# Ninety-six scatters that wait for TensorE, and centroid products and gate logits in column groups

## The chip, the cores and the metric

The kernel runs on one core of one Trainium2 chip. A core has TensorE (PE; its weight loads are listed apart as PEld), VectorE (DVE), ScalarE (ACT), GpSimd (POOL) and SyncE (SP), each with its own queue of instructions, and 16 DMA engines. The metric is the time of one execution on the device in microseconds, lower being better. All inputs and the output are float32.

## The reference

The reference is a chain of three parts. The third takes its gate and its skip score from the second's output.

```
q_assign = argmax(q_n @ c_n, -1)                 # q_n, k_n, c_n: rows of length 1; 16 centroids per head
k_assign = argmax(k_n @ c_n, -1)
mask = q_assign[:, :, :, None] == k_assign[:, :, None, :]
scores = where(mask, q @ k.T / sqrt(64), -1e9)   # 2 batches, 8 heads, 768 tokens, head size 64
attn = softmax(scores) @ v
x = attn, heads side by side                     # 1536 tokens of 512
h = x @ w_in                                     # 512 -> 2048
x = where(h > 0, h, exp(h) - 1) @ w_out          # 2048 -> 512
skip_score = x @ w_skip                          # only tokens with a score above 0 go on, the others are copied
logits = x @ w_gate                              # 8 experts
e = argmax(logits); gate_w = softmax(logits)[e]
out = x + gate_w * (relu(x @ w1[e]) @ w2[e])     # 512 -> 1024 -> 512
```

## The kernel before

**Heads go in pairs**, two heads of 64 on 128 partitions, four pairs for each batch. The two batches are worked in different ways.

Batch 0 is *dense*: its four pairs (n = 0 to 3) compute all 768 x 768 scores, and the mask is added by rows of one-hot clusters under the head's 64 rows. Its steps in the order table are `scores`, `peak`, `exp`, `flip` (three transposes of the exponentials by PE into one bank, L519), `head` (ACT rounds them to fp32r, `ptH`, L531), `rest` (DVE subtracts that from them, `ptL`, L537), `pv` (the products with V). ACT's `head` needs PE's `flip`, DVE's `rest` needs `head`, and the next `flip` into the same bank needs `rest`.

Batch 1 is *sorted*: for each of its four pairs (j = 0 to 3) the rows of q, k and v are put in the order of their clusters, so that later only blocks near the diagonal are computed. The clusters come from centroid products (`sort_similar`, L712 to 718), the largest of 16 (`sort_max`), running sums (`scum`, `srank`) and an index for each token (`sidx`). Then 24 indirect DMAs per pair, issued by POOL, write each token's row to its place in DRAM: `sort_scatter`, L767 to 776, steps `sc0a` to `sc5d`, for chunks of 128 tokens (0 to 5), q or k with v, head 0 or 1, into the tensors `qs` and `kvs`. That makes 96 scatters. Before them SP fills `kvs` with zeros (`zero`), and SP loads the rows (`sload`); behind the last ones the sorted rows are read back (`bload0` to `bload7`) and the block attention runs (`tq` to `nm`), whose results 48 gathers on POOL bring back to token order (`og`, L868).

**The order is written out by hand.** `attention()` (L1131) goes through a table ORDER of 1902 step names ("sc3a:0" is a scatter of pair 0, "head2b:1" a `head` of dense pair 1) and calls each step's function; each engine gets its instructions in the order in which the steps stand. The table holds everything up to the second half of the FFN (`cv`, `h`, `e`, `y`, `z` steps: weights split into two parts, products, ELU). A scatter stands 1 to 47 steps behind the one before. Between engines only data dependencies make anyone wait; a scatter waits for its index, its row load, the zero fill and the scatter eight ahead of it on its DMA semaphore.

**Centroid products of the dense pairs.** `similar` (L393 to 401) multiplies q and k by the centroids in three fp32r passes (`cwH` times the head `T[nm, "H"]` and the rest `T[nm, "L"]`, `cwL` times the head), for each half of the tokens: 12 matmuls of 64 columns of weights and 384 moving columns, L399. `similar_out` copies each half to `rows`, and `turn_back` (L405) transposes six pieces of 64 rows. A bank then holds, for each chunk of 128 tokens, four groups of 16 similarities (L408).

**Centroid products of the sorted pairs.** `sort_similar` takes the turned tokens as weights (128 columns) and the 32 centroid columns `cwF` as what moves: 12 float32 matmuls, L716, straight into the layout that `sort_max` reads.

**The gate.** `route` takes each tile of 128 FFN output tokens, turns it (`turn`, L1445) and multiplies it by `wgs` (gate and skip weights, 16 columns): `logits`, L1449 to 1454, four float32 matmuls into one 128 x 16 accumulator and a copy by DVE. For batch 1's last tiles the steps stand in a second table, TAIL: T turns, L makes logits, C chooses the expert, R ranks, h is held back work of TensorE (the last FFN products), x fetches tokens, F fills slots. The routed experts follow (L1683 to 1768).

Of the kernel before, what the change touches and what calls it, by code (L numbers as in the profile page):

```python
# [10 lines left out]
F32 = mybir.dt.float32  # L11
# [23 lines left out]
TAIL = ("h3 h3 h3 T0 T2 h3 L0 T1 h5 L2 L1 T3 h5 C0 h4 h4 R0 h4 h4 x- T4 h5 L3 L4 C3 h5 x0 T5 R3 x2 L5 x4 F0 C5 R5 N5 x3 x1 x5 F5 F3").split()  # L35
# [8 lines left out]
NEAR = 4  # L44
BY_DVE = 16, 16
# [4 lines left out]
    turnq0:0 THq0:0 turnq1:0 TLq0:0 THq1:0 turnk0:0 TLq1:0 THk0:0 turnk1:0 TLk0:0 THk1:0 TLk1:0 simq0:0 simk0:0 loadqk:0 sT0:0  # L50
    simq1:0 simk1:0 sT1:0 back:0 sv:0 mx:0 eqsub:0 turnq0:1 rawq0:1 first:0 THq0:1 turnq1:1 TLq0:1 least:0 rawq1:1 THq1:1
    equal:0 TLq1:1 rows:0 moveT0:0 moveO0:0 oT:0 turnk0:1 rawk0:1 THk0:1 moveT1:0 turnk1:1 TLk0:1 rawk1:1 THk1:1 TLk1:1 vtH:0
    vtL:0 sload0:0 sload1:0 bank scores0a:0 scores0b:0 scores1b:0 peak0:0 exp0:0 scores1a:0 scores2a:0 peak1:0 scores2b:0
    flip0a:0 exp1:0 flip0b:0 head0a:0 scores3a:0 head0b:0 peak2:0 rest0a:0 scores3b:0 rest0b:0 flip1a:0 moveO1:0 flip1b:0 exp2:0
    head1a:0 scores4a:0 peak3:0 scores4b:0 head1b:0 rest1a:0 exp3:0 suq0:0 pv0a:0 flip2a:0 rest1b:0 pv0b:0 head2a:0 flip2b:0
    pv0c:0 rest2a:0 scores5a:0 seq0:0 suq1:0 head2b:0 peak4:0 scores5b:0 seq1:0 peak5:0 flip3a:0 simq0:1 exp4:0 simk0:1 pv0d:0
    zero:0 scores6b:0 sT0:1 suk0:0 rest2b:0 head3a:0 flip3b:0 pvlow0:0 rest3a:0 pvsum0:0 scores6a:0 sek0:0 flip4a:0 head3b:0
    simq1:1 exp5:0 rest3b:0 simk1:1 peak6:0 head4a:0 sT1:1 flip4b:0 rest4a:0 scores7a:0 suk1:0 loadv:0 head4b:0 flip5a:0
    scores7b:0 sek1:0 back:1 exp6:0 rest4b:0 sv:1 flip5b:0 peak7:0 sload0:1 scores8a:0 mx:1 scores8b:0 head5a:0 ssim0:0 eqsub:1
    ssim1:0 pv1a:0 rest5a:0 pv1c:0 peak8:0 pv1b:0 flip6a:0 pv1d:0 head5b:0 exp7:0 scores9b:0 first:1 exp8:0 rest5b:0 scores10a:0  # L60
    least:1 smx:0 vtH:1 flip6b:0 sone:0 head6a:0 pvlow1:0 scum:0 srank:0 pvsum1:0 pv2a:0 rest6a:0 flip7a:0 pv2c:0 equal:1 pv2b:0
    head7a:0 vtL:1 pv2d:0 moveT0:1 scores9a:0 sidx:0 rows:1 head6b:0 rest6b:0 flip7b:0 sc2c:0 rest7a:0 pvlow2:0 peak9:0 oT:1
    flip8a:0 loadqk:1 head7b:0 pvsum2:0 rest7b:0 exp9:0 scores10b:0 turnq0:2 peak10:0 pv3a:0 pv3b:0 pv3c:0 scores11b:0 sc3b:0
    scores11a:0 sc4b:0 THq0:2 TLq0:2 flip8b:0 turnq1:2 sc0d:0 head8a:0 sc5a:0 rest8a:0 exp10:0 moveO0:1 flip9a:0 head8b:0
    scores0a:1 peak11:0 THq1:2 head9a:0 scores0b:1 rest8b:0 pv3d:0 TLq1:2 flip9b:0 rest9a:0 exp11:0 turnk0:2 flip10a:0 head9b:0
    rest9b:0 pvlow3:0 pvsum3:0 scores1b:1 scores1a:1 head10a:0 flip10b:0 sc0a:0 pv4a:0 rest10a:0 flip11a:0 THk0:2 peak0:1
    sload1:1 sc3a:0 TLk0:2 pv4b:0 pv4c:0 head10b:0 rest10b:0 head11a:0 exp0:1 pv4d:0 suq0:1 seq0:1 flip11b:0 scores2a:1 sc2d:0
    sc1b:0 pvlow4:0 rest11a:0 flip0a:1 turnk1:2 peak1:1 pvsum4:0 head11b:0 THk1:2 exp1:1 rest11b:0 TLk1:2 scores2b:1 pv5a:0
    peak2:1 invert:0 head0a:1 pv5b:0 flip0b:1 suq1:1 zero:1 pv5c:0 scores3a:1 seq1:1 sc4d:0 scores3b:1 simq0:2 head0b:1 rest0a:1
    exp2:1 sc2a:0 simk0:2 sc1a:0 flip1a:1 rest0b:1 peak3:1 flip1b:1 scores4a:1 sT0:2 head1a:1 scores4b:1 rest1a:1 moveT1:1  # L70
    suk0:1 exp3:1 sc5b:0 pv5d:0 flip2a:1 sc1c:0 peak4:1 moveO1:1 sek0:1 loadv:3 head1b:1 scores5a:1 sc5c:0 simq1:2 sc0b:0 smem:0
    simk1:2 head2a:1 exp4:1 rest1b:1 scores5b:1 flip2b:1 scores6b:1 sT1:2 head2b:1 rest2a:1 loadv:1 pvlow5:0 suk1:1 flip3a:1
    peak5:1 scores6a:1 rest2b:1 sc1d:0 sek1:1 flip3b:1 back:2 sumT:0 exp5:1 scores7a:1 pvsum5:0 sc2b:0 head3a:1 peak6:1 rest3a:1
# [91 lines left out]
class _Core:  # L165
# [26 lines left out]
    def first_loads(self):  # L192
# [1778 lines left out]
```

## Time and profile before

| | |
|---|---|
| time, median of 3 runs | 749.87 us (747.6 to 751.81) |
| the profiled execution | 748.56 us |
| its span on the core | 746.8 us |
| PE busy | 635.4 us, 85% |
| PEld busy | 576.0 us, 77% |
| DVE busy | 431.6 us, 58% |
| ACT busy | 392.9 us, 53% |
| POOL busy | 271.7 us, 36% |
| mean granted clock of TensorE | 0.921 |

The profile is one execution. Its span runs from the first to the last instruction; the execution's own time is 1.8 us more. Busy shares are means over stages that differ: attention, FFN and experts. The granted clock is the share of TensorE's full clock that the chip allowed.

### The profile page before, as it was taken

How to read it: one execution, taken by the hardware profiler on the slowest of the kernel's cores; microseconds unless marked ns; L12 is line 12 of the kernel's file. 1: busy time of each engine (PE TensorE's matmuls, PEld its weight loads, DVE VectorE, ACT ScalarE, POOL GpSimd, SP SyncE). 2: the span in 40 equal slices, each digit the busy share in tenths (PEclk: the TensorE clock that was granted, in tenths of full speed). 3: DMA queues.
4: the chain of work that ended last, by engine and by line, in shares of the span. 5: the costliest groups of instructions: out<-in, count | busy, mean ns of one | idle time of the engine just before them, and what ended most of it. 6: DMA issues, size and time to landing. Idle time of an engine off the chain costs nothing.

```text
span 746.8 us, 11604 instructions
## 1 busy us (share of the span) xinstructions
PE 635.4 (85%) x3988; PEld 576.0 (77%) x3988; DVE 431.6 (58%) x982; ACT 392.9 (53%) x850; POOL 271.7 (36%) x289
## 2 busy tenths in 40 slices
PE   5991892874772399999999999999999999999996
PEld 3881882773662399888989889999998988999995
DVE  6680790872660398999698775333245545135663
ACT  4761770852641398776776765544544622124552
POOL 3247067047057302865664352323223203121101
PEclk9795896897695599999999999999999999999999
DMA  7877064576331039666654553642421027989960
GB/s 174 208 172 195 14 156 112 129 159 165 91 90 37 22 101 251 183 178 199 204 180 154 165 161 101 254 169 61 165 57 57 14 110 266 384 291 319 335 231 18
DMA packets 99957, 118.30 MB, mean 158 GB/s; under 512 B 47553, under 2 KB 68209, under 8 KB 99888
## 3 DMA queue, kind: packets, MB, share of 16 engines
q1 hardware_dynamic: 92080, 106.70, 47.4%
q0 software_dynamic: 6096, 10.34, 4.3%
q8 instruction: 33, 0.54, 0.3%
q10 hardware_dynamic: 1712, 0.43, 0.3%
q14 instruction: 36, 0.29, 0.1%
HBM read 80.17 MB, written 27.80 MB: 145 GB/s over the span
## 4 chain that ended last, share of the span: by engine, by line
PE 65%; DVE 11%; another core or an unknown queue 11%; ACT 6%; issue 3%; DMA 1%; SPq 0%; POOL 0%; POOLq 0%; ACTq 0%; DVEq 0%
PE ps_p L1269 7%; PE ps_v L1269 6%; PE ps_t L1720 5%; PE ps_t L519 4%; PE ps_p L1735 4%; PE ps_v L1735 4%; PE ps_v L550 4%; PE ps_sB L1308 3%; PE ps_sA L1308 3%; PE ps_t L1308 3%; PE ps_sA L498 2%; PE ps_sB L498 2%; PE ps_sA L1325 2%; DVE cv_b L1217 1%
## 5 line engine op out<-in xcount | busy, mean ns | idle before, releaser
L519 PE MATMUL ps_t<-ident,pe 128*128 128x128 f32 x288 | 53.5, 307 | 59.9 <-issue 30.4
L519 PEld LDWEIGHTS ps_t<-ident,pe 128*128 128x128 f32 x288 | 38.6, 159 | 66.8 <-issue 32.8
L531 ACT ACTIVATE ptH<-ps_t 128x384 fp32r<-128x384 f32 x96 | 46.0, 491 | 82.5 <-remote 59.0
L537 DVE TENSOR_TENSOR ptL<-ps_t,ptH 128x384 fp32r<-128x384 f32 x96 | 52.1, 551 | 58.9 <-ACT ptH L531 45.7
L868 POOL DMA_INDIRECT og<-od,idx x48 | 51.2, 1066 | 55.2 <-ACT rp L830 27.8
L1223 POOL TENSOR_TENSOR r<-cv_b,cv_t 128x512 int32<-128x512 int32 x32 | 42.9, 1341 | 47.5 <-DVE cv_b L1217 19.7
L550 PE MATMUL ps_v<-ptH,vt 128*128 128x256 f32 x144 | 44.0, 328 | 14.6 <-issue 8.6
L1269 PE MATMUL ps_p<-xH,w1H 128*128 128x384 f32 x128 | 44.3, 346 | 1.9 <-DVE gL L1297 1.5
L1768 POOL DMA_INDIRECT out_dram<-o,dest x10 | 11.0, 1104 | 93.4 <-DVE o L1766 92.8
L1293 DVE SCALAR_TENSOR_TENSOR ps_p<-e,ps_p 128x384 f32<-128x384 f32 x32 | 17.9, 560 | 45.1 <-ACT e L1291 45.1
L550 PEld LDWEIGHTS ps_v<-ptH,vt 128*128 128x128 f32 x144 | 30.7, 215 | 16.6 <-issue 9.3
L1269 PE MATMUL ps_v<-xH,w1H 128*128 128x384 f32 x124 | 42.0, 339 | 1.3 <-DVE gL L1297 1.3
L1269 PE MATMUL ps_p<-xL,w1H 128*128 128x384 f32 x128 | 43.0, 336 | 0.0
L550 PE MATMUL ps_v<-ptL,vt 128*128 128x256 f32 x144 | 41.5, 312 | 0.3 <-DVE ptL L537 0.3
L1269 PE MATMUL ps_v<-xL,w1H 128*128 128x384 f32 x124 | 41.6, 335 | 0.0
L1249 POOL TENSOR_TENSOR w2L<-r,w2H 128x512 fp32r<-128x512 f32 x12 | 15.3, 1279 | 71.5 <-PE ps_t L1308 57.4
L1289 ACT ACTIVATE e<-ps_p 128x384 f32<-128x384 f32 x32 | 15.7, 490 | 40.7 <-PE ps_p L1269 40.7
L770 POOL DMA_INDIRECT kvs<-rowsH,idx x24 | 23.8, 990 | 33.8 <-DVE idx L755 23.1
L1735 PE MATMUL ps_p<-xs,ew 128*128 128x128 f32 (+2 forms) x256 | 35.4, 280 | 0.5 <-ACT xs L1683 0.5
L1735 PEld LDWEIGHTS ps_p<-xs,ew 128*128 128x128 f32 x256 | 33.7, 191 | 2.3 <-ACT xs L1683 0.6
L1735 PEld LDWEIGHTS ps_v<-xs,ew 128*128 128x128 f32 x256 | 33.7, 191 | 1.8
L1735 PE MATMUL ps_v<-xs,ew 128*128 128x128 f32 (+2 forms) x256 | 35.0, 279 | 0.0
(491 smaller groups left out, 2006.7 us busy)
## 6 DMA issues: line engine op xcount, KB each, us to landing
ew<-in_moe_w_dram SPq DMA_DIRECT2D x32, 1024.0 KB
d<-in_moe_w_in_dram SPq DMA_DIRECT2D x16, 512.0 KB
d<-in_moe_w_out_dram SPq DMA_DIRECT2D x16, 512.0 KB
wf_d<-r SPq DMA_DIRECT2D x16, 512.0 KB
r<-wf_d SPq DMA_DIRECT2D x16, 512.0 KB
zk<-kvs SPq DMA_DIRECT2D x8, 520.0 KB
KA<-kH SPq DMA_DIRECT2D x16, 192.0 KB
kvs<-zeros SPq DMA_DIRECT2D x8, 325.0 KB
```

Of the source, the lines that this page charges most:

```text
L498: self.nc.tensor.matmul(self.sc[u][:, half, 0:384], lhsT=d["Q" + a][0:rows, c * 128:c * 128 + 128], rhs=d["K" + a][0:rows, half * 384:half ...
L519: self.nc.tensor.transpose(ps[:, 0, j * 128:j * 128 + 128], self.pe[u][:, half, j * 128:j * 128 + 128], self.ident)
L531: self.nc.scalar.activation(self.split(u, half)[0], self.tp[u, half][:, 0, 0:384].rearrange("p (c q) -> p c q", c=3), AF.Copy)
L537: self.nc.vector.tensor_tensor(l, self.tp.pop((u, half))[:, 0, 0:384].rearrange("p (c q) -> p c q", c=3), h.bitcast(F32), ALU.subtract)
L550: self.nc.tensor.matmul(self.vp[n, j], lhsT=self.vt[n][:, j // NG, c, :], rhs=t, start=(part == 0 and i == 0), stop=(part == 3 and i == 2 ...
L770: store = self.nc.gpsimd.indirect_dma_start(dst[2 * j + h], bass.IndirectOffsetOnAxis(ap=self.idx[:, j, 4 * c + r:4 * c + r + 1], axis=0), ...
L868: self.nc.gpsimd.indirect_dma_start(self.og[j][:, c, h, :], None, self.o_d[i], bass.IndirectOffsetOnAxis(ap=self.idx[:, j, 4 * c + h:4 * c ...
L1223: G.tensor_tensor(r[:, j * 512:j * 512 + 512].bitcast(I32), b, self.cvt.pop((f, j)), ALU.add)
L1269: self.nc.tensor.matmul(ps, lhsT=w[:, c, :], rhs=x[:, c, :], start=(i == 0), stop=(i == 11))
L1308: self.nc.tensor.matmul(self.y[bl][part][t], lhsT=a[:, t * 128:t * 128 + 128], rhs=w, start=(f == 0 and i == 0), stop=(f == NF - 1 and i = ...
L1720: PE.matmul(y[0][0:W], lhsT=a, rhs=b, start=(f == 0 and i == 0), stop=(f == NF - 1 and i == 2))
L1735: PE.matmul(ps[:, 0:W], lhsT=w1[:, c, i * 128:i * 128 + 128], rhs=xs[:, c, 0:W], start=(c == 0), stop=(c == 3))
```

## The change

**A wait for each scatter.** `sort_scatter` calls a new function `follow`, which makes the scatter depend on the TensorE instruction that stands fourteen TensorE instructions ahead in the flat order of the program (FOLLOW = 14).

**A new table.** ORDER is written anew: 1890 steps. The scatters now stand 5 to 22 steps apart, 9 or 10 mostly. Everything around them moves a little too: zero fills, row loads, V's low part, the centroid steps.

**Centroid products in four column groups.** A dense pair's twelve matmuls become eight with the float32 centroids `cwF` (32 columns) as weights: q and k of both halves go to four different quarters of the partitions of one bank, head first, then rest on top. One copy (`similar_out`, to `simT`) and three full transposes follow, where there were two and six. A sorted pair's twelve matmuls become four of the same form with the turned tokens moving, a copy by ACT (`sTT`) and three transposes (`sback`). The groups of 16 similarities stand in another order afterwards, and `group` and `index` say where. `cwH` and `cwL` go.

**Gate logits in four column groups.** Each of the four pieces of a turned tile is multiplied into its own quarter, with the weights `wgs`, now 32 wide, loaded and 128 tokens moving. A copy, one transpose and a sum over the four quarters by DVE (`back`, steps B0 and B3 in TAIL) follow, held over to the next tile. The last tile of batch 1 keeps the old form. `second_ops` asks for the low weights of the second FFN product only where they are used.

```diff
 TAIL:
-"h3 h3 h3 T0 T2 h3 L0 T1 h5 L2 L1 T3 h5 C0 h4 h4 R0 h4 h4 x- T4 h5 L3 L4 C3 h5 x0 T5 R3 x2 L5 x4 F0 C5 R5 N5 x3 x1 x5 F5 F3"
+"h3 h3 h3 T0 T2 h3 L0 T1 h5 L2 h5 L1 T3 h4 B0 C0 h4 h4 h4 x- R0 T4 h5 L3 h5 L4 x0 B3 C3 T5 x2 L5 R3 x4 F0 C5 R5 N5 x3 x1 x5 F5 F3"
+FOLLOW = 14
 ORDER = """
...
-    sload1:1 sc3a:0 TLk0:2 pv4b:0 pv4c:0 head10b:0 rest10b:0 head11a:0 exp0:1 pv4d:0 suq0:1 seq0:1 flip11b:0 scores2a:1 sc2d:0
...
+    pvsum3:0 exp11:0 turnk0:2 rest10a:0 pv4a:0 sc4d:0 moveO1:1 peak0:1 pv4b:0 THk0:2 pv4c:0 head10b:0 flip11a:0 TLk0:2 zero:1
...
-    def similar(self, n, nm, half):
...
-        for j, (w, x) in enumerate(((self.cwH, "H"), (self.cwH, "L"), (self.cwL, "H"))):
-            self.nc.tensor.matmul(self.sim[n, half][0:64, 0:384], lhsT=w[:, p, o:o + 64], rhs=self.T[n][nm, x][:, cs],
-                                  start=(nm == "q" and j == 0), stop=(nm == "k" and j == 2))
...
+    def similar(self, n):
...
+        for x in "HL":
+            for i, (half, nm) in enumerate(itertools.product(range(2), "qk")):
+                self.nc.tensor.matmul(ps[32 * i:32 * i + 32, 0:384], lhsT=self.cwF[:, p, :],
+                                      rhs=T[nm, x][:, half * 384:half * 384 + 384].bitcast(F32), start=(x == "H"), stop=(x == "L"))
+
+    def similar_out(self, n):
+        self.simT = self.sort_tile("sT", [128, 384], F32)
+        self.nc.scalar.activation(self.simT, self.sim.pop(n)[:, 0:384], AF.Copy)
...
     def turn_back(self, n):
         ps = self.back[n] = self.bank_p()
-        for c in range(self.NC):
-            self.nc.tensor.transpose(ps[:, c * 64:c * 64 + 64], self.rows[0:64, c * 128:c * 128 + 128], self.ident[0:64, 0:64])
+        for c in range(3):
+            self.nc.tensor.transpose(ps[:, c * 128:c * 128 + 128], self.simT[:, c * 128:c * 128 + 128], self.ident)
...
-        for c in range(3 * half, 3 * half + 3):
-            for i, nm in enumerate("qk"):
-                o = c * 64 + 32 * i
-                self.nc.tensor.matmul(self.ssim[:, o:o + 32], lhsT=self.sT[j, nm][:, c * 128:c * 128 + 128],
-                                      rhs=self.cwF[:, j, :], start=True, stop=True)
+    def sort_similar(self, j):
+
+        ps = self.ssims = self.bank_p()
+        for i, (half, nm) in enumerate(itertools.product(range(2), "qk")):
+            self.nc.tensor.matmul(ps[32 * i:32 * i + 32, 0:384], lhsT=self.cwF[:, j, :],
+                                  rhs=self.sT[j, nm][:, half * 384:half * 384 + 384], start=True, stop=True)
...
+    def group(self, c):
+        return c % 3 * 8 + c // 3 * 4
+
+    def index(self, j, c, r):
+        g = self.group(c) + r
+        return self.idx[:, j, g:g + 1]
+
     def sort_scatter(self, j, c, r):
...
         store = self.nc.gpsimd.indirect_dma_start(
-            dst[2 * j + h], bass.IndirectOffsetOnAxis(ap=self.idx[:, j, 4 * c + r:4 * c + r + 1], axis=0),
+            dst[2 * j + h], bass.IndirectOffsetOnAxis(ap=self.index(j, c, r), axis=0),
             self.sort_rows(j, c // 3)[:, c % 3, lo:hi], None, bounds_check=1023, oob_is_err=False)
+        self.follow(store)
...
+    def follow(self, store):
+
+        done = [i for i in self.nc.cur_bb.bb.instructions if i.engine == mybir.EngineType.PE][-FOLLOW]
+        self.tc.add_manual_dep(store.ins, done.name, mybir.DependencyInfo(mybir.DependencyClass.Sync, mybir.DependencyReason.DATA),
+                               reason="scatters keep step with TensorE")
...
         def logits(t):
...
             for j in range(4):
-                PE.matmul(lp, lhsT=x2T[:, j * 128:j * 128 + 128], rhs=self.wgs[:, j, :],
-                          start=(j == 0), stop=(j == 3))
-            V.tensor_copy(lg[:, t, :], lp)
+                PE.matmul(lp[32 * j:32 * j + 32, 0:128], lhsT=self.wgs[:, j, :], rhs=x2T[:, j * 128:j * 128 + 128],
+                          start=True, stop=True)
+            before = back(lp)
+            lgT = fw.tile([128, 128], F32, tag="lgT", bufs=2, name="lgT")
+            (S.copy if b else V.tensor_copy)(lgT, lp[:, 0:128])
+            held["back"] = t, lgT
+            before()
```

**POOL, before, the end of the scatters of pair 0 and the start of pair 1's.** `qs` and `kvs` are the sorted tensors in DRAM, `rowsH` and `rowsL` the loaded rows, DMASW a scatter of POOL itself, DMAHW a load or fill of SP, `eq` the similarities of a dense pair and `vt` the low part of V:

```order
L770 DMA qs_191<-rowsH,idx 1024x64 [waits DMASW1_49]
L770 DMA kvs_198<-rowsH,idx 1024x130 [waits DMASW2_49]
L429 TENSOR_TENSOR eq<-eq,mx 128x384 [waits DVE_49]
L770 DMA kvs_199<-rowsL,idx 1024x130 [waits DMASW3_49]
L770 DMA qs_190<-rowsL,idx 1024x64 [waits DMASW4_49]
L490 TENSOR_TENSOR vt<-natv,vt 128x12x64 [waits DMAHW2_49,DMAHW3_49,PE_49,Activation_49]
L770 DMA kvs_198<-rowsL,idx 1024x130 [waits DMASW5_49]
L770 DMA kvs_199<-rowsL,idx 1024x130 [waits DMASW6_49]
L770 DMA kvs_198<-rowsL,idx 1024x130 [waits DMASW7_49]
L770 DMA kvs_200<-rowsL,idx 1024x130 [waits DMAHW1_49,DMAHW0_49,DMAHW7_49,DMASW0_49,DVE_49]
L770 DMA qs_193<-rowsL,idx 1024x64 [waits DMAHW0_49,DMASW1_49]
L770 DMA kvs_201<-rowsH,idx 1024x130 [waits DMAHW1_49,DMASW2_49]
```

**POOL, after, the same place:**

```order
L778 DMA kvs_195<-rowsH,idx 1024x130 [waits DMASW7_49,PE_49]
L778 DMA kvs_195<-rowsH,idx 1024x130 [waits DMASW0_49,PE_49]
L778 DMA kvs_194<-rowsL,idx 1024x130 [waits DMASW1_49,PE_49]
L425 TENSOR_TENSOR eq<-eq,mx 128x384 [waits DVE_49]
L778 DMA qs_187<-rowsL,idx 1024x64 [waits DMASW2_49,PE_49]
L778 DMA qs_187<-rowsL,idx 1024x64 [waits DMASW3_49,PE_49]
L778 DMA kvs_194<-rowsH,idx 1024x130 [waits DMASW4_49,PE_49]
L778 DMA qs_186<-rowsH,idx 1024x64 [waits DMASW5_49,PE_49]
L778 DMA qs_187<-rowsH,idx 1024x64 [waits DMASW6_49,PE_49]
L778 DMA qs_186<-rowsL,idx 1024x64 [waits DMASW7_49,PE_49]
L486 TENSOR_TENSOR vt<-natv,vt 128x12x64 [waits DMAHW3_49,DMAHW2_49,Activation_49]
L778 DMA qs_188<-rowsH,idx 1024x64 [waits DMAHW5_49,DMASW0_49,DMAHW6_49,DVE_49,PE_49]
```

Each scatter carries a wait for PE now, beside the waits that it had. The subtraction of the largest similarity (L429, now L425) and V's low part (L490, now L486) stand among the scatters as before.

**PE, before, the centroid products of the first dense pair**, behind the transposes of its q and k (`ps_p`, `ps_v`, `ps_t` are banks of PSUM):

```order
L399 MATMUL ps_p<-qH,cwH 64x384 [waits DVE_49]
L399 MATMUL ps_p<-qL,cwH 64x384
L399 MATMUL ps_p<-qH,cwL 64x384
L399 MATMUL ps_p<-kH,cwH 64x384 [waits Activation_49]
L399 MATMUL ps_p<-kL,cwH 64x384 [waits DVE_49]
L399 MATMUL ps_p<-kH,cwL 64x384
L399 MATMUL ps_v<-qH,cwH 64x384 [waits PE_49]
L399 MATMUL ps_v<-qL,cwH 64x384
L399 MATMUL ps_v<-qH,cwL 64x384
L399 MATMUL ps_v<-kH,cwH 64x384 [waits Activation_49]
L399 MATMUL ps_v<-kL,cwH 64x384 [waits DVE_49]
L399 MATMUL ps_v<-kH,cwL 64x384
```

**PE, after, the same place**, with the three transposes back:

```order
L394 MATMUL ps_p<-qH,cwF 32x384 [waits DVE_49]
L394 MATMUL ps_p<-kH,cwF 32x384 [waits Activation_49]
L394 MATMUL ps_p<-qH,cwF 32x384
L394 MATMUL ps_p<-kH,cwF 32x384 [waits Activation_49]
L394 MATMUL ps_p<-qL,cwF 32x384
L394 MATMUL ps_p<-kL,cwF 32x384 [waits DVE_49]
L394 MATMUL ps_p<-qL,cwF 32x384
L394 MATMUL ps_p<-kL,cwF 32x384 [waits DVE_49]
L404 MATMUL ps_v<-ident,ssT 128x128 [waits Activation_49]
L404 MATMUL ps_v<-ident,ssT 128x128 x2
```

Twelve matmuls of 64 columns of weights in two banks became eight of 32 columns in one bank; the six transposes of L408 that stood behind them became three.

## Rows read from the trace of the kernel before

**Rows 1.** The page's chain that ended last, shares of the span by engine.

```profile
PE 65%; DVE 11%; another core or an unknown queue 11%; ACT 6%; issue 3%; DMA 1%; SPq 0%; POOL 0%; POOLq 0%; ACTq 0%; DVEq 0%
```

**Rows 2.** The table of stretches, busy time of each engine in each stretch.

```profile
core 0: us, PE busy (x) PEld busy (x) DVE busy (x) ACT busy (x) POOL busy (x), PEclk, DMA share, GB/s
...
49.00:75.50 26.50, 9.77 (x60) 7.90 (x59) 6.87 (x12) 6.52 (x14) 18.66 (x19) 0.67 0.63 167
75.50:106.80 31.30, 29.10 (x206) 27.00 (x206) 27.25 (x56) 23.12 (x53) 7.73 (x7) 0.89 0.37 86
106.80:132.00 25.20, 10.42 (x63) 8.91 (x63) 6.78 (x13) 6.72 (x15) 17.75 (x18) 0.69 0.38 102
132.00:168.00 36.00, 30.76 (x208) 27.88 (x209) 29.33 (x59) 25.39 (x57) 8.50 (x8) 0.89 0.63 149
168.00:192.00 24.00, 9.69 (x60) 8.15 (x58) 5.66 (x11) 5.73 (x12) 15.57 (x16) 0.70 0.69 177
192.00:211.50 19.50, 18.21 (x122) 17.15 (x122) 16.55 (x35) 14.69 (x35) 0.00 (x0) 0.84 0.12 29
211.50:254.00 42.50, 12.07 (x71) 10.25 (x70) 9.57 (x20) 8.05 (x17) 30.13 (x31) 0.62 0.21 65
254.00:280.00 26.00, 25.56 (x198) 24.05 (x198) 21.25 (x56) 22.01 (x53) 1.05 (x2) 0.89 0.28 72
...
305.00:600.00 295.00, 289.69 (x1554) 260.32 (x1553) 184.49 (x360) 177.97 (x359) 126.56 (x104) 1.00 0.44 141
600.00:746.00 146.00, 138.89 (x1018) 129.28 (x1018) 68.13 (x212) 50.58 (x124) 21.32 (x20) 0.99 0.70 250
```

**Rows 3.** The timeline of 50 to 80 us: start, duration, engine, work, [idle before].

```profile
61.73 0.90 PE L519 MATMUL ps_t<-ident,pe 128*128 128x128 f32 x3 [0.54 <-issue]
...
72.24 0.97 POOL L770 DMA_INDIRECT kvs<-rowsH,idx  x1 [0.30 <-issue]
...
75.56 0.49 ACT L531 ACTIVATE ptH<-ps_t 128x384 fp32r<-128x384 f32 x1 [13.60 <-remote]
...
76.70 0.90 PE L519 MATMUL ps_t<-ident,pe 128*128 128x128 f32 x3 [12.79 <-DVE ptL L537]
```

**Rows 4.** The scatters' line L770: ns min/median/max, first and last start, idle before.

```profile
L770 POOL DMA_INDIRECT qs<-rowsL,idx x24: 971/972/978, 50.5 to 249.8; - x24
...
  issue: 27.0, 90
```

**Rows 5.** The same timeline at the start of the first stall.

```profile
49.07 1.16 POOL L770 DMA_INDIRECT kvs<-rowsH,idx  x1 [4.00 <-DMA natq<-in_q_dram]
...
51.12 0.56 DVE L537 TENSOR_TENSOR ptL<-ps_t,ptH 128x384 fp32r<-128x384 f32 x1 [0.22 <-ACT ptH L531]
...
53.09 0.97 POOL L770 DMA_INDIRECT kvs<-rowsH,idx  x1 [0.31 <-issue]
```

**Rows 6.** The waits of 150 to 161 us: us in total, times, longest.

```profile
DVE st L504 <- remote: 2.2, 1, 2.2
DVE smx L724 <- PE ps_t L519: 1.8, 1, 1.8
```

**Rows 7.** The chain's pieces in order of time: start, us, work.

```profile
35.36 1.04 PE ps_p L399 x6
...
152.18 1.27 PE ps_p L716 x12
...
604.00 0.89 PE ps_v L1453 x8
604.90 0.48 PE ps_p L1445 x4
...
626.39 0.89 PE ps_p L1735 x8
```

**Rows 8.** The sorted pairs' centroid products, line L716, columns as in rows 4.

```profile
L716 PE MATMUL ps_p<-cwF,sT x96: 193/276/276, 39.9 to 203.9; 128*128 128x32 f32 x96
```

**Rows 9.** The timeline of 120 to 129 us.

```profile
123.90 0.49 ACT L531 ACTIVATE ptH<-ps_t 128x384 fp32r<-128x384 f32 x1 [2.39 <-remote]
...
127.42 0.49 ACT L531 ACTIVATE ptH<-ps_t 128x384 fp32r<-128x384 f32 x1 [3.03 <-PE ps_sA L498]
```

More of the change, by code (lines that the diff above doesn't have):

```diff
@@ L49 @@
 ORDER = """
[L50 to L53, printed above, removed]
@@ L58 @@
[L58 to L61, printed above, removed]
@@ L1449, in logits, with back @@
         def logits(t):
-            lp = bank()[:, 0:16]
+            lp = bank()
             x2T = held.pop(t)
-            for j in range(4):
-                PE.matmul(lp, lhsT=x2T[:, j * 128:j * 128 + 128], rhs=self.wgs[:, j, :],
-                          start=(j == 0), stop=(j == 3))
-            V.tensor_copy(lg[:, t, :], lp)
+            if nt == 1:
+                for j in range(4):
+                    PE.matmul(lp[:, 0:16], lhsT=x2T[:, j * 128:j * 128 + 128], rhs=self.wgs[:, j, 0:16],
+                              start=(j == 0), stop=(j == 3))
+                V.tensor_copy(lg[:, t, :], lp[:, 0:16])
+                return
+            for j in range(4):
+                PE.matmul(lp[32 * j:32 * j + 32, 0:128], lhsT=self.wgs[:, j, :], rhs=x2T[:, j * 128:j * 128 + 128],
[5 more added lines that the diff above has]
+            before()
+        def back(ps=None):
+            if "back" not in held:
+                return lambda: None
+            t, lgT = held.pop("back")
+            if ps is None:
+                ps = bank()
+            PE.transpose(ps[:, 128:256], lgT, self.ident)
+            add = lambda: V.tensor_reduce(lg[:, t, :], ps[:, 128:256].rearrange("p (j e) -> p e j", j=4)[:, 0:16, :], axis=AX.X, op=ALU.add)
+            return add
         def choose():
@@ L1499, in route @@
         return ([lambda t=t: copy(t) for t in range(nt)], [lambda t=t: turn(t) for t in range(nt)],
-                [lambda t=t: logits(t) for t in range(nt)], choose, rank, fill)
+                [lambda t=t: logits(t) for t in range(nt)], lambda ps=None: back(ps)(), choose, rank, fill)
     def first_fetch(self):
@@ L1551, in route_beside @@
         yield
-        for _, turn, logits, choose, rank, fill in halves:
+        for _, turn, logits, back, choose, rank, fill in halves:
             for i in range(3):
@@ L1557, in route_beside @@
                 yield
+            back(self.ps("p")[:, 0, :])
             choose()
@@ L1577, in route_last @@
         for c0, ys in ((0, y[0]), (3, y[1][0:2]), (5, y[1][2:3])):
-            copy, turn, logits, choose, rank, fill = self.route(b, c0, ys, bank)
+            copy, turn, logits, back, choose, rank, fill = self.route(b, c0, ys, bank)
             for i in range(len(ys)):
-                steps["c", c0 + i], steps["T", c0 + i], steps["L", c0 + i] = copy[i], turn[i], logits[i]
+                for x, f in zip("cTL", (copy, turn, logits)):
+                    steps[x, c0 + i] = f[i]
+            steps["B", c0] = back
             steps["C", c0], steps["R", c0], steps["F", c0] = choose, rank, fill
```

269 lines of the change are left out of this document (135 added, 134 removed).

## The prediction, on record before the changed kernel ran

> **What bounds the kernel now.** I read the shares of the chain first, then the table of stretches, then the timeline inside one stretch. The chain that ends last is 65% TensorE, but 11% of it, some 80 us, stands under "another core or an unknown queue", on a kernel that has one core [rows 1]. The stretches say where that is. Up to 280 us ordinary stretches and stretches in which PE, DVE and ACT all stand still alternate; in each of the latter POOL runs its scatters one behind the other (19, 18, 16 and 31 POOL instructions) [rows 2]. They are 26.5 + 25.2 + 24.0 + 42.5 = 118.2 us. From 305 us on PE is busy 290 of 295 us and 139 of 146 us [rows 2]: that part is TensorE's and the first edit cannot shorten it.
>
> Inside one stall: PE issues three transposes at 61.73 us; ACT, which needs only their signal, gets it at 75.56, after 13.60 us, a little over 2 us behind the end of the last scatter of the row; DVE waits for ACT, and PE's next transposes, at 76.70, for DVE [rows 3]. Nothing was computed late there: the signal from PE was. The scatters take 0.97 us each, and 90 of the 96 start 0.30 us (27.0/90) after the one before, so the period is 1.27 us [rows 4]. The first four of that row (49.07 to 53.09) hurt nobody: DVE's low-part subtractions run beside them at 0.56 us [rows 5].
>
> So the present order table, which sets the scatters one to some tens of steps apart, is not what POOL does: no scatter waits for another engine once the indices are there, POOL runs through them as fast as it can, and it is the closed row of scatters that PE's signals do not get past.
>
> **The change, part by part.**
>
> *The wait.* Every scatter now waits for the TensorE instruction fourteen ahead of it in the written order, and the new table puts mostly 8 to 12 steps between scatters. Counted in the two built programs, the new one has 946 TensorE matmuls from the first to the last scatter, so 10 between two scatters on the average, 0 to 27 single; the rows of scatters without any wait are gone. In ordinary stretches PE passes 206 + 208 + 122 + 198 = 734 recorded instructions in 112.8 us, 6.5 per us [rows 2], so ten are 1.54 us, against the 1.27 us that a scatter needs: POOL has about 17% to spare, and short rows of two or three remain where the table sets them close.
>
> Worth: the four stalled stretches hold 60 + 63 + 60 + 71 = 254 PE instructions, 39.0 us at 6.5 per us; by DVE, 28.9 us busy at the ordinary stretches' 0.84 (94.4 of 112.8), 34.5 us [rows 2]. I take the longer: 118.2 - 39.0 = **79 us gained**; the other gives 84. PE's lower clock in the stalls (0.62 to 0.70) is inside this, since I count instructions, not busy time.
>
> What is late next: nothing else is near. POOL's 96 scatters are 122 us of the some 152 that remain from 49 to 280 us, and the DMA engines' share there rises from 0.41 (the mean of those eight stretches) to 0.63 [rows 2]. Queued behind a waiting scatter on POOL are the subtraction of the largest similarity and the low part of V (twice each) and other scatters; a scatter waits for one point of PE, so these come later by a step or two of 1.5 us, and the table has other work for DVE in between. The rows of one head pair are read back only after the last pair's indices exist, far behind. Zero fills and row loads move a few steps on SP's queue; at 0.63 I cost that at nothing, and at some 3 us if a load is late once.
>
> *What remains of the stalls.* Bounds: nothing, from the four scatters in a row that hurt nobody [rows 5]; and 4.0 us for six in a row at 152 us, where DVE waits 1.8 and 2.2 us on PE's signals [rows 6], so 0.67 us per scatter, 64 us in all. The new spacing gives rows of two or three, nearer to the first: I take 0.1 us each, **10 us back**.
>
> *Centroid products.* Dense pairs: twelve 384-column matmuls, six in 1.04 us, so 2.1 us per pair, become eight exact f32 ones of 32 columns of weights that write four different quarters. An f32 matmul is two recorded instructions (the 48 matmuls of L716 are 96 rows), of 0.11 us for 128 columns (eight in 0.89 us) [rows 7, 8]; with 384 columns it is 0.67 us. Eight are 5.3 us if the quarters take turns, 1.3 us if four run at once. Sorted pairs: 24 rows at 0.106 us (twelve in 1.27), 2.5 us, become four matmuls, 2.7 or 0.67 us, and three transposes (four in 0.48), 0.36 us [rows 7]. Over four pairs of each: between -9 and +15 us of PE work. No row shows quarters at work, so I take the middle of what stands beside other work, **0**, and keep both ends. On ACT one copy of a dense pair goes and one of a sorted pair comes: nothing.
>
> The Trainium skill says (TensorEngine Tiling (Array Packing), Key Properties) that changing the tiling mode drains TensorE. No run here shows it; an estimate from rows is the 276 ns that an f32 instruction of L716 lasts less the 0.11 us at which the next follows [rows 7, 8], 0.17 us, and 38 changes of mode would be 6 us. By that the sum would be 6 us longer.
>
> *Gate logits.* Per tile of 128 tokens, 8 rows of 0.11 us (0.89 us) become 8 in turn or a quarter of it, and a transpose of 0.12 us [rows 7]. Eleven tiles (the twelfth keeps its form) lie where PE is nearly always busy: +1.3 to -6 us, I take **-2**. The added copy and sum per tile are DVE's or ACT's, which are free there; in the tail they stand before a choice of expert, and cost 2 to 3 us if the held matmuls do not cover them. The second FFN product only asks for its low weights later: nothing.
>
> **Sum.** 746.8 - 79 + 10 + 0 - 2 = 675.8 us of span. The profiled execution took 748.56, 1.8 over its span, and the median of the runs shown is 749.87, 1.3 over that: **679 us**.
>
> **Rivals.**
>
> 1. *The stall comes back in small change.* 1.54 us is not far from 1.27, and where PE runs fast POOL falls behind, its wait is then met already and it runs closed again. For it: six in a row cost 0.67 us each [rows 6]. Against it: a PE whose signal is held up also holds up the next scatter, which the old kernel had not. At 0.67 us: 746.8 - 79 + 64 - 2 + 3 = 733 us.
> 2. *Slower: every scatter holds PE's signal until its data have landed, close or not.* In the stall at 121 to 127 us ACT gets one signal after 2.39 and one after 3.03 us of waiting, one per two to three scatters [rows 9]. Spread over the whole stage, 96 scatters would meet a working PE each time, and at a full period of 1.27 us lost each they take 122 us where the rows now lose 79: 746.8 + 43 - 2 + 3 = 791. It decides from 79/96 = 0.82 us per scatter on. Against it: the four at 49 us [rows 5] cost nothing.
> 3. *No change:* what is lost is a fixed time per scatter wherever it stands. 96 times 0.97 us is 93 us, near the 79, so time would stay near 750. The Trainium skill gives such a mechanism (SBUF — State Buffer, Who interferes with whom): DVE and GpSimd lock a shared port pair for a whole instruction, the other blocked. Against it in the trace: the first to wait is ACT, on PE [rows 3], and DVE is not slowed beside scatters [rows 5]. The same holds if POOL, late by its indices, never meets its wait.
> 4. *More than forecast:* quarters run at once (-9, -6) and ordinary stretches grow denser, so under 650.
>
> **How the numbers follow.** Forecast (650 to 705) 0.65; rival 1 (705 to 734) 0.15; rival 2, or the dearer products with no cover, slower, 0.09; rival 3 0.06; rival 4 0.05. The range takes the forecast and nearly all of rival 1: 650 to 734. About 0.5% is what a measurement of this kernel can tell. Faster: 0.65 + 0.15 + 0.05 = 0.85; within 0.5%: 0.06; slower: 0.09.
>
> **What would show it.** Right: scatters about 1.5 us apart, ending with waits on TensorE in place of 0.30 us "issue"; no stretch of 5 us with PE, DVE and ACT all idle before the FFN; the chain's unknown share near 1%; the granted clock near 1.0 through that part; the first FFN matmul some 70 us earlier; from there on the same time as before within 5 us. The products: L394 and L708 with neighbours that start closer than 0.11 us if quarters overlap. Wrong: "remote" waits of ACT and DVE of the old total in more pieces (rival 1 or 3), or longer (rival 2); row loads late behind SP's moved fills; POOL without waits, closed rows again.

## The result and the profile after

The changed kernel took 676.5 us (median of 4 runs, 673.6 to 679.6) against 749.4 us for the kernel before: a ratio of 0.902, with an interval of 0.899 to 0.905. The forecast was 679. The profiled execution took 673.6 us, its span is 671.8 us.

The page's chain by engine, to be held against [rows 1]:

```profile
PE 71%; DVE 13%; issue 4%; DMA 4%; ACT 3%; SPq 2%; another core or an unknown queue 1%; POOL 0%; POOLq 0%; DVEq 0%; ACTq 0%
```

The unknown share fell from 11% to 1%. The stretches, columns as in [rows 2]:

```profile
49.00:80.00 31.00, 28.02 (x205) 23.05 (x204) 26.04 (x49) 23.88 (x57) 20.89 (x22) 1.00 0.73 187
80.00:110.00 30.00, 25.78 (x187) 21.96 (x190) 26.09 (x51) 22.44 (x52) 18.49 (x19) 1.00 0.76 195
...
200.00:230.00 30.00, 25.42 (x175) 23.99 (x173) 17.10 (x56) 19.13 (x46) 16.42 (x17) 0.77 0.62 168
...
300.00:530.00 230.00, 227.97 (x1230) 199.56 (x1229) 123.87 (x254) 130.97 (x260) 79.89 (x63) 1.00 0.39 130
530.00:671.00 141.00, 133.08 (x975) 123.59 (x973) 66.60 (x209) 49.47 (x123) 21.62 (x20) 0.98 0.70 248
```

Stretches with 19 to 22 POOL instructions are now busy ones; before, PE, DVE and ACT stood still in such stretches. From the first scatter until 3 us after the last, the time in which all three are idle is 3.0 us in all, where the kernel before has 63.1. The first FFN matmul (L1284, before L1269) starts at 237.0 us instead of 311.5, and from there to the end both kernels take 435 us (434.8 and 435.3). The whole gain lies ahead of the FFN. The busy time of each engine from 49 us to the first FFN matmul, before and after, columns as in [rows 2]:

```profile
49.00:311.50 262.50, 175.51 (x1245) 160.05 (x1244) 150.84 (x340) 139.80 (x320) 114.73 (x115) 0.80 0.46 120
```

```profile
48.60:237.00 188.40, 164.26 (x1203) 143.12 (x1201) 148.68 (x340) 139.66 (x320) 115.62 (x114) 0.95 0.64 166
```

PE's idle time there fell from 87 to 24 us, and its busy time from 176 to 164 us, with 42 instructions fewer and the granted clock at 0.95 instead of 0.80.

The scatters (line L778, before L770), columns as in [rows 4]:

```profile
L778 POOL DMA_INDIRECT qs<-rowsL,idx x24: 969/972/1324, 48.6 to 206.5; - x24
...
  issue: 17.8, 55
  PE ps_v L546: 9.1, 9
```

From first to last they take 160.5 us, 1.69 us each; 54 of the 95 distances are still the closed 1.28 us, in rows of two to four. Behind such a row an engine still waits now and then. From the timeline of 82 to 88 us:

```profile
84.50 0.82 PE L515 MATMUL ps_t<-ident,pe 128*128 128x128 f32 x6
84.64 1.06 POOL L778 DMA_INDIRECT qs<-rowsL,idx  x1 [0.31 <-issue]
...
86.66 0.87 ACT L527 ACTIVATE ptH<-ps_t 128x384 fp32r<-128x384 f32 x2 [2.93 <-PE ps_p L445]
```

All six of PE's transposes were over by 85.3 us; ACT, idle for 2.93 us, starts on the first three at 86.66.

### The profile page after: what moved, and what is told of

It reads as the page before. It is cut to its first block, busy times and chain, and to the rows that moved or that the text cites. A ratio compares the mean times of both kernels' runs of the same rounds, so it can differ in the third digit from the quotient of the medians.

```text
span 671.8 us, 11614 instructions
## 1 busy us (share of the span) xinstructions
PE 621.0 (92%) x3951; PEld 547.8 (82%) x3951; DVE 430.3 (64%) x984; ACT 394.3 (59%) x853; POOL 275.6 (41%) x289
## 4 chain that ended last, share of the span: by engine, by line
PE 71%; DVE 13%; issue 4%; DMA 4%; ACT 3%; SPq 2%; another core or an unknown queue 1%; POOL 0%; POOLq 0%; DVEq 0%; ACTq 0%
PE ps_v L1284 8%; PE ps_p L1284 7%; PE ps_t L1758 5%; PE ps_t L515 4%; PE ps_p L1773 4%; PE ps_v L1773 4%; PE ps_sB L1323 4%; PE ps_sA L1323 4%; PE ps_t L1323 4%; PE ps_v L546 3%; PE ps_sA L494 2%; PE ps_sB L494 2%; PE ps_sA L1340 2%; PE ps_t L1340 2%; PE ps_sB L1340 2%
## 5 line engine op out<-in xcount | busy, mean ns | idle before, releaser
L515 PE MATMUL ps_t<-ident,pe 128*128 128x128 f32 x288 | 47.6, 284 | 7.6 <-DVE ptL L533 5.2
L515 PEld LDWEIGHTS ps_t<-ident,pe 128*128 128x128 f32 x288 | 34.9, 145 | 15.5 <-issue 6.9
L1284 PE MATMUL ps_p<-xH,w1H 128*128 128x384 f32 x128 | 44.4, 347 | 1.6 <-DVE gL L1312 1.2
L1284 PE MATMUL ps_p<-xL,w1H 128*128 128x384 f32 x128 | 43.0, 336 | 0.0
L1284 PE MATMUL ps_v<-xH,w1H 128*128 128x384 f32 x124 | 42.1, 340 | 0.9 <-DVE gL L1312 0.9
L1284 PE MATMUL ps_v<-xL,w1H 128*128 128x384 f32 x124 | 41.6, 336 | 0.0
L546 PE MATMUL ps_v<-ptH,vt 128*128 128x256 f32 x144 | 39.0, 299 | 0.5 <-issue 0.4
L546 PE MATMUL ps_v<-ptL,vt 128*128 128x256 f32 x144 | 38.5, 293 | 0.0
L1306 ACT ACTIVATE e<-e 128x384 f32<-128x384 f32 x64 | 33.5, 524 | 1.7
L778 POOL DMA_INDIRECT kvs<-rowsL,idx x24 | 23.9, 996 | 17.1 <-PE ps_v L546 4.3
```

What stands on the lines that cost most here:

```text
L515: self.nc.tensor.transpose(ps[:, 0, j * 128:j * 128 + 128], self.pe[u][:, half, j * 128:j * 128 + 128], self.ident)
L546: self.nc.tensor.matmul(self.vp[n, j], lhsT=self.vt[n][:, j // NG, c, :], rhs=t, start=(part == 0 and i == 0), stop=(part == 3 and i == 2 ...
L1284: self.nc.tensor.matmul(ps, lhsT=w[:, c, :], rhs=x[:, c, :], start=(i == 0), stop=(i == 11))
L1306: S.activation(e, e, AF.Exp, scale=-1.0)
```

## The experiments

Three sets of four kernels ran, each set on one chip together with the kernel before. A ratio is to the kernel before on the same chip.

**First set: what of the change is it?** The kernel before took 751.2 us there. The changed kernel beside the others:

> The changed kernel once more, beside the three below on one chip, so that they can be compared with it directly. All theories: 674 to 680 us, 0.90 of the kernel before.

Measured: 676.9 us, 0.900 (0.898 to 0.903).

*Without the wait:*

```diff
             self.sort_rows(j, c // 3)[:, c % 3, lo:hi], None, bounds_check=1023, oob_is_err=False)
-        self.follow(store)
```

> The changed kernel without the wait of the scatters for TensorE; table, centroid products and gate logits stay new. Theory (the wait is what spaces the scatters; a table alone cannot, since POOL runs ahead of it): closed rows at 1.28 us return, the stalls with them, 730 to 755 us. Rival (the new table spaces them, by the places of the indices, fills and loads): within 10 us of the changed kernel, so under 690. Between the two, 690 to 730: both share.

Measured: 748.7 us, 0.999 (0.996 to 1.002). The wait carries all of it: 72 us against the changed kernel of this set. Without it the scatters stand in closed rows again (17, 6, 17, 7, 16, 17 and 11), and the stalls are back. The chain, and the stretches with the scatters' rows in it:

```profile
PE 60%; DVE 13%; another core or an unknown queue 8%; issue 6%; ACT 6%; DMA 4%; SPq 1%; POOL 0%; POOLq 0%; DVEq 0%; ACTq 0%
```

```profile
48.00:75.00 27.00, 9.08 (x58) 7.26 (x55) 7.62 (x14) 6.94 (x16) 17.71 (x18) 0.71 0.79 182
...
108.00:130.00 22.00, 6.17 (x36) 5.41 (x35) 4.62 (x8) 3.68 (x9) 14.81 (x16) 0.63 0.45 113
...
214.00:249.00 35.00, 10.48 (x46) 8.30 (x46) 6.22 (x11) 6.57 (x14) 22.61 (x23) 0.58 0.15 47
```

The new table sets the scatters evenly, and that alone does nothing: POOL runs ahead of a table as soon as it has nothing to wait for. The new products and logits are in this kernel too and do not show in its time.

*With the old centroid products* (the bodies of `similar`, `similar_out`, `turn_back` and `sort_similar` of the kernel before, `group(c)` = 4 c):

```diff
+    def similar_out(self, n):
+        self.similar_out_half(n, 0)
+        for nm in "qk":
+            self.similar_half(n, nm, 1)
+        self.similar_out_half(n, 1)
...
     def group(self, c):
-        return c % 3 * 8 + c // 3 * 4
+        return 4 * c
```

> The changed kernel with the old centroid products of both kinds of pairs (twelve fp32r matmuls and six transposes per dense pair, twelve float32 ones per sorted pair, the second half of a dense pair's behind the copy of the first since the table has one step for both). In the changed kernel's trace four quarters start within 0.02 us and the next four 0.33 us later, so they run at once: a dense pair takes some 1.4 us instead of 2.1, a sorted pair 0.85 and 0.55 for three transposes instead of 2.5, some 7 us of PE work in all. Theory (PE sets the pace between 49 and 260 us, 0.88 busy): 4 to 9 us longer than the changed kernel. Rival (it stood beside waits for ACT, DVE and the scatters): within 2 us of it.

Measured: 682.2 us, 0.908 (0.905 to 0.912). That is 0.008 over the changed kernel, some 6 us (3 to 9 by the two intervals): what the new products are worth here. The old ones had to wait for a copy between their halves in this kernel, which the old table did not ask for, so 6 us is more likely too much than too little.

*With the old logits:*

```diff
-            if nt == 1:
+            if nt >= 1:
                 for j in range(4):
```

> The changed kernel with the old form of the gate logits in all twelve tiles (four matmuls of 128 columns of weights, 16 moving, one accumulator; no copy, transpose and sum). In the changed kernel's trace the eight instructions of a tile take some 0.3 us and a transpose 0.11, against 0.89 before. Theory (that stage is PE's, 99% busy): eleven times 0.5, 4 to 6 us longer than the changed kernel. Rival (the copy and sum in the tail, before the choice of expert, give it back): within 2 us of it.

Measured: 681.1 us, 0.905 (0.902 to 0.909), 0.005 over the changed kernel, some 4 us; by the two intervals it may be anything up to 7. It rests on the two longest of six executions (683.7 and 687.9 us); the other four, 671.7 to 681.3, lie among the changed kernel's own, 674.6 to 682.7. And this kernel keeps the new TAIL, which was written for the new logits, so it doesn't say what the logits are worth against the kernel before.

**Second set: what about the wait does it?** The kernel before took 758.7 us on this second chip. The changed kernel wasn't run there; its 0.900 of the first set stands in for it. The ranges expected below were set for a kernel before of some 750 us, so a time on this chip is held against them by its ratio too.

*The kernel before with the wait alone:*

```diff
+        self.follow(store)
         before = self.stores.setdefault((kv, 2 * j + h), [])
```

> The kernel before with the wait alone: each scatter waits for the TensorE instruction fourteen ahead of it in the old table, whose scatters stand 1 to 47 steps apart; products and logits old. Theory (the wait does it, wherever the table sets the scatters, short rows cost little): the gain but for the products and logits (5 and 4 us by the two kernels that undo them) and some 10 us for rows the old table sets close, 685 to 705 us. Rival (wait and spacing are each worth much): 710 to 735.

Measured: 708.1 us, 0.932 (0.929 to 0.936): slightly over the theory's range and under the rival's, but 700 us by its ratio on the first chip, inside the theory's. It is 0.032, some 24 us, behind the changed kernel. At most 6 of these are the centroid products; the logits count for nothing here, since this kernel has the old TAIL with them. So an estimate of some 18 us, across two chips, belongs to the table. Its rows reach seven and ten scatters, where the old table sets them close.

*POOL spread by itself, without any wait:*

```diff
-        self.follow(store)
+        for i in range(2):
+            self.nc.gpsimd.memset(self.spare, 0.0)
```

> The changed kernel without the wait, but with two clears of a spare 128 x 256 tile on POOL ahead of each scatter, some 0.6 us: scatters are spread to a period of some 1.9 us, by POOL itself and not by TensorE. Theory (PE's signals only need a gap between scatters): at 1.9 us the stalls go, under 690 us. Rival (what holds the signals is POOL's row itself, or each scatter until it has landed; it ends only when the next scatter cannot start before PE's signal has come): 730 to 790 us.

Measured: 711.9 us, 0.938 (0.935 to 0.942), between the two. By the edit the clears stand behind each scatter, not ahead of it; either way they part one from the next. The scatters stand 2.08 us apart, with 1.1 us between the end of one and the start of the next, and no signal of PE is held any more: where an engine waited for one given beside a scatter, it came within 0.04 us. Three long stretches remain in which PE, DVE and ACT all stand still, 41.5 us together, of another kind. The waits of 49 to 258 us (us in total, times, longest):

```profile
DVE eq L430 <- POOL eq L425: 27.7, 2, 15.8
...
PE ps_v L824 <- DMA zk<-kvs: 24.6, 2, 21.6
```

DVE waits for the subtraction of the largest similarity, which stands on POOL's queue behind scatters, and PE for the sorted rows, whose last scatters come at 256 us. POOL with 200 us of scatters is simply late. So a gap is enough, but the gap must not cost POOL its time.

*Scatters that wait for DVE:*

```diff
-        done = [i for i in self.nc.cur_bb.bb.instructions if i.engine == mybir.EngineType.PE][-FOLLOW]
+        done = [i for i in self.nc.cur_bb.bb.instructions if i.engine == mybir.EngineType.DVE][-4]
```

> The changed kernel with the scatters waiting for the VectorE instruction four ahead in the flat order, in place of the TensorE instruction fourteen ahead. Theory (any engine that works through the flat order paces POOL as well): 672 to 690 us. Rival (it has to be TensorE's signal, the one that is held up): over 700.

Measured: 693.6 us, 0.914 (0.910 to 0.918): over the theory's range and under the rival's, but 687 us by its ratio on the first chip, inside the theory's. Nearly nine tenths of the gain come without a wait on PE, so it need not be PE's signal. What is missing, some 10 us, comes with rows of up to five; that they cost it is not shown. Whether another distance on DVE would do as well as PE wasn't tried.

*A looser wait* (`FOLLOW = 60`):

> The changed kernel with the wait for the TensorE instruction sixty ahead: POOL may run some six scatters ahead of the table before it must stop. Theory (only long rows hurt, six in a row cost 4 us in the kernel before): rows of up to six after each pause, 680 to 715 us. Rival (rows of two to four are already as dear per scatter): same as the changed kernel, within 4 us; or, if a row once begun keeps PE's signals away and so itself alive, over 730.

Measured: 713.0 us, 0.938 (0.934 to 0.943), nearly four tenths of the gain gone, as the theory has it. Rows of seven, eight and ten appear, and with them the old kind of wait, which ACT's `ptH` copies no longer have in the changed kernel. From the waits of 49 to 255 us:

```profile
ACT ptH L527 <- remote: 20.1, 6, 4.4
```

**Third set: how small may the gap be, and can the rest be had?** This set ran on a third chip, and there the question doesn't arise: the expectation of 0.90 failed.

> The changed kernel once more, beside the three below on their chip: 0.90 of the kernel before.

Measured: the kernel *before* takes 645.3 us on this chip (23 runs, 643.9 to 647.6; 747 to 753 and 757 to 760 on the others), the changed kernel 643.7, a ratio of 0.997 (0.995 to 0.999). The trace of the changed kernel shows what is different. POOL falls behind the table, finds its waits met, and runs in closed rows, four of them of 12, 11, 12 and 21, and nobody waits for that. The chain, then a stretch in the middle of the row of 21 (143.0 to 168.6 us), then the timeline inside it:

```profile
PE 66%; DVE 15%; DMA 6%; ACT 6%; issue 3%; SPq 3%; POOL 1%; POOLq 0%; DVEq 0%; ACTq 0%
```

```profile
140.00:170.00 30.00, 29.74 (x239) 27.59 (x238) 28.19 (x66) 26.72 (x61) 22.30 (x23) 1.00 0.53 143
```

```profile
157.06 0.97 POOL L778 DMA_INDIRECT kvs<-rowsL,idx  x1 [0.30 <-issue]
157.06 0.82 PE L515 MATMUL ps_t<-ident,pe 128*128 128x128 f32 x6
...
157.73 0.85 ACT L527 ACTIVATE ptH<-ps_t 128x384 fp32r<-128x384 f32 x2
...
158.34 0.97 POOL L778 DMA_INDIRECT kvs<-rowsH,idx  x1 [0.30 <-PE ps_p L574]
...
159.62 0.97 POOL L778 DMA_INDIRECT kvs<-rowsL,idx  x1 [0.30 <-PE ps_t L515]
```

ACT takes up PE's transposes while scatter follows scatter at 1.28 us. The kernel before was timed on this chip but not traced; its granted clock of 0.988, against 0.92 on the other chips, fits a kernel without stalls, but no trace of it shows that.

*One clear instead of two, no wait:*

```diff
-        self.follow(store)
+        for i in range(1):
+            self.nc.gpsimd.memset(self.spare, 0.0)
```

> The changed kernel without the wait, with one clear of a spare 128 x 256 tile on POOL ahead of each scatter instead of two: a period of some 1.7 us, so 0.7 us between scatters instead of the 1.1 that the two clears made. With two clears no stall came from a held signal of PE; the 44 us left were waits for POOL's own queue, which was late. Theory (a gap of 0.7 us lets PE's signals past too, and POOL at 1.7 us is no later than in the changed kernel, where 96 scatters take 160 us): 0.90 to 0.92 of the kernel before. Rival (0.7 us are not enough): held signals as without any wait, 0.95 to 1.0.

Measured: 654.6 us, 1.014 (1.012 to 1.016). Neither theory can be put to the test, since the changed kernel's trace shows no signal held on this chip. It shows the price of POOL's time: a period of 1.46 us, the last scatter at 198.0 us instead of 186.7, and 11 us more than the changed kernel of this set.

*The wait and one clear:*

```diff
         self.follow(store)
+        self.nc.gpsimd.memset(self.spare, 0.0)
```

> The changed kernel with its wait, and one clear of a spare 128 x 256 tile on POOL ahead of each scatter: rows of two to four scatters at 1.28 us, of which the changed kernel still has some thirty, become scatters at 1.7 us. Theory (what is left of held signals, 13 us of long waits on ACT, goes): 3 to 10 us shorter than the changed kernel. Rival (POOL, now 163 us for the scatters, is late with the last ones): 2 to 15 us longer.

Measured: 655.8 us, 1.015 (1.013 to 1.018), the same price. Whether it would gain where signals are held stays open.

*A tighter wait* (`FOLLOW = 4`):

> The changed kernel with the wait for the TensorE instruction four ahead instead of fourteen: each scatter starts some ten instructions, 1.5 us, later, and POOL can run ahead of the table by less than one scatter. Theory (rows of two to four get shorter, nobody waits for a single scatter): 0 to 6 us shorter than the changed kernel. Rival (POOL loses its slack and the subtraction of the largest similarity and the low part of V, which stand behind waiting scatters, come late): 2 to 10 us longer.

Measured: 646.0 us, 1.001 (0.999 to 1.003), 2.4 us over the changed kernel, as the rival has it; that POOL's lost slack is the cause is not shown. What shorter rows would give on the other chips can't be seen on this one.

No kernel tried here is clearly faster than the changed one. On the first chip its ratio is the lowest, with the old logits too close behind to part; on the second, where it wasn't run, none comes down to its 0.900; on the third it is 0.3% ahead of the kernel before.

## Why the forecast came out right, and what in it was wrong

**The cause was right, on the chips where the stalls are.** They were closed rows of scatters that PE's signals did not get past, and the wait ends them: no wait, no gain (0.999). The traces let one say more than the prediction did. I took every case in which an engine stood waiting for a single signal of another engine that had been given inside a row of five or more scatters, and the time from the end of the instruction that gave it to the start of the one that waited:

| | signals of PE | signals of ACT | signals of DVE |
|---|---|---|---|
| before | 19: median 1.7 us, longest 12.9 | 19: at most 0.06 | 8: at most 0.06 |
| changed, no wait | 19: median 1.1 us, longest 7.4 | 13: at most 0.05 | 13: at most 0.06 |
| changed, FOLLOW 60 | 20: median 0.4 us, longest 5.9 | 14: at most 0.05 | 5: at most 0.06 |
| changed, third chip | 19: at most 0.04 | 7: at most 0.05 | 2: at most 0.05 |

Of the three, only PE's signals are held. The ends of PE's instructions are modelled in the trace, so what comes late may be the signal or the end of the work that it tells of; nothing here parts the two. What is plain is that PE had taken up its next matmuls: in the first stall the transposes begin at 61.73 us [rows 3], and this begins behind them:

```profile
63.39 0.52 PE L498 MATMUL ps_sB<-KB,QB 80*128 80x384 f32 x1
```

That only PE's signals are held is why DVE's subtractions ran undisturbed at 51 us [rows 5], while ACT, which needs PE, waited 13.6 us [rows 3].

**The sum came out right; its two terms are in doubt.** The wait was put at 79 us gained and 10 given back, 69 together; it measured 72 (748.7 against 676.9). But 10 us may not be what the holds still cost. The same program needs 33 us less on the third chip (643.7 against 676.9), all of it ahead of the FFN: its first FFN matmul starts at 203.9 us instead of 237.0, and the rest takes 439 us against 435. Two stretches of its trace, up to 170 us and up to the first FFN matmul:

```profile
49.00:170.00 121.00, 117.65 (x905) 104.49 (x905) 115.11 (x242) 106.10 (x242) 89.98 (x89) 1.00 0.75 189
...
49.00:203.90 154.90, 151.55 (x1210) 138.08 (x1210) 145.81 (x338) 138.21 (x321) 115.26 (x114) 1.00 0.78 202
```

Beside the changed kernel's row in the section on the result: for about as many PE instructions, 3 us of PE idle instead of 24, and 13 us less of PE busy, at a granted clock of 1.00 instead of 0.95. If nothing else differs between the chips, which no run shows, and all of it is the holds, they cost 0.34 us per scatter in the changed kernel, not 0.1, and some 106 us in the kernel before, not 79. Both terms would then be some 25 us too small, and that the errors cancelled would be luck.

By that measure the step that failed is the choice of "ordinary" stretches as the yardstick. They are not what this work takes without stalls. PE passed 6.5 instructions per us in them; on the third chip, with scatters all the way, it passes 905 in 121 us, 7.5 per us. Two things differ. PE is busy 0.141 us per instruction in them against 0.130, at a granted clock of 0.84 to 0.89 [rows 2] against 1.00; the prediction allowed for the lower clock in the stalls and not for this one. And PE stands idle for 8% of them against 3%, with the held signals at 152 us [rows 6] inside one. Held signals are not all of it: from 192 to 211.5 us no scatter runs, and PE passes 6.3 per us at 0.84 [rows 2]. The older products are in them too, so no run gives the shares.

What the changed kernel still loses is to be seen in ACT's idle time ahead of the 96 `ptH` copies, on the page after and on that of the third chip (busy, mean ns, then idle before):

```profile
L527 ACT ACTIVATE ptH<-ps_t 128x384 fp32r<-128x384 f32 x96 | 45.2, 491 | 24.0 <-PE ps_t L515 8.1
```

```profile
L527 ACT ACTIVATE ptH<-ps_t 128x384 fp32r<-128x384 f32 x96 | 45.2, 492 | 9.2 <-PE ps_t L515 7.6
```

Without the wait it is 73.2 us, 40.5 of them "remote".

**The bounds for a scatter held.** The 0.34 us, if it is that, lies between 0 and 0.67. I had put the value near the lower end because the new spacing was to give short rows; it did (mostly two to four), and by the third chip they are dearer than the first four scatters at 49 us made them look. The period was to be 1.54 us and is 1.69.

**Centroid products: 0 forecast, 6 us gained** (3 to 9). The open point was whether quarters run at once. They do. The four sorted products of one pair, eight instructions, and what follows, from the timeline of 38.5 to 40.8 us:

```profile
39.21 0.33 PE L494 MATMUL ps_sA<-KB,QB 80*128 80x384 f32 x1
39.48 0.85 PE L708 MATMUL ps_p<-sT,cwF 128*32 128x384 f32 x8
40.26 0.38 PE L546 MATMUL ps_v<-ptH,vt 128*128 128x256 f32 x1
```

Eight instructions take 0.85 us; single starts are 0.006 us apart within four, and the next four start 0.35 us after the first. One after the other they would have been 2.7 us, the old form was 2.5 [rows 7]. The middle of two bounds was the wrong choice for an unknown that has two values and no middle. The first product starts 0.26 us behind the last matmul ahead of it, where those stand 0.18 apart, and the next matmul starts 0.42 us behind the last product, where the second four start 0.33 us behind the last of the first. That is 0.09 us for a change of form, half of the 0.17 that the prediction estimated, some 3 us for the 38 changes. The Trainium skill says that a change of tiling mode drains TensorE (TensorEngine Tiling (Array Packing), Key Properties); these starts agree with it.

**Gate logits: 2 us forecast, none gained that shows.** All of them lie behind the first FFN matmul, and from there on both kernels take 435 us. A tile's eight instructions let the next one start 0.36 us after the first of them (409.23 and 409.59), against 0.89 for the old eight [rows 7]:

```profile
409.23 0.42 PE L1474 MATMUL ps_v<-x2T,wgs 128*32 128x128 f32 x8
409.59 0.33 PE L1488 MATMUL ps_v<-ident,lgT 128*128 128x128 f32 x1
409.67 0.42 PE L1284 MATMUL ps_p<-xH,w1H 128*128 128x384 f32 x1
```

From the first logit matmul to the last it is 139.7 us instead of 142.4, so 2.7 us are saved. But from there to the first expert product it is 9.4 us instead of 6.5. The prediction named a cost of that size, "2 to 3 us if the held matmuls do not cover them", and left it out of the sum. It put it down to the added copy and sum; but with the old logits in the new TAIL the two times are 143.0 and 10.7 us, so by one execution of each kernel the loss goes with the new TAIL, whatever the form, and the 4 us of that kernel are measured in a tail that was not its own.

**The rivals.** The first (the stall comes back in small change, because POOL falls behind and runs closed again) may describe part of the truth: 33 us of it if all that the third chip saves is holds, not 64. On that chip POOL does fall behind, for 21 scatters in a row, and it costs nothing. The second (each scatter holds a signal by itself) is refuted by the kernel with two clears, in which signals beside single scatters came within 0.04 us. The third (a fixed time per scatter wherever it stands) is refuted by the change itself: the same 96 scatters, and 73 us less. The fourth (denser stretches, under 650) is what the third chip shows with its 643.7, but there without a gain.

**The signs named ahead** came true where they concern the stalls: the unknown share at 1%, no idle stretch of 5 us ahead of the FFN, the first FFN matmul 74.5 us earlier, the time behind it unchanged. So did the products': L394 and L708 have neighbours 0.006 us apart. Two did not: 55 of the scatters still end in "issue", not in a wait on TensorE, and the clock is not near 1.0 throughout (0.77 from 200 to 230 us, where DVE and ACT too are busy less than two thirds of the time).

**What the prediction did not ask** is whether the stall belongs to the kernel or to the chip it ran on. The forecast holds in the comparison above and in the first set; on the third chip the same two kernels differ by 0.3%, where the range forecast 2 to 13%. What differs on that chip (its state, its load or its set-up) stays open. So does why, of three engines, only PE's signals are held. One more lesson for the next forecast: the quiet stretches of a stalled kernel are no yardstick for a kernel without stalls before their granted clock and their waits have been read.

## What to carry to other kernels

Where engines stand idle under "remote" or an unknown queue while GpSimd issues indirect DMAs one behind the other, try tying each DMA to a point in the working engine's order: an order table alone does not hold back a queue that waits for nothing. Give it a wait and not filler work, since the queue's own later instructions, and whoever reads what the DMAs wrote, pay for filler. And time such a kernel on more than one chip before counting the gain: here it was 10% on one and 0.3% on another.

## What the hardware showed beyond the forecast

- Beside indirect DMAs at 1.28 us, on two chips, signals of TensorE were held up to 12.9 us, while signals of ScalarE and VectorE came within 0.06 us. With 1.1 us between two DMAs none was held.
- The effect is not on every chip: 751 and 759 us for the kernel before on two, 645 us on a third, where TensorE's signals pass rows of 21 indirect DMAs within 0.04 us.
- Exact float32 matmuls of 32 columns of weights that write four different quarters of the partitions start 0.006 us apart and run at once (eight instructions of 384 columns in 0.85 us). Going from full matmuls to these and back adds 0.09 us each time.
